# Earlier weights, a DMA transpose, one q buffer and a finer last tile in an attention and FFN kernel

## The chip, the cores and the metric

The kernel runs on one core of one Trainium2 chip. The metric is the time of one execution in device microseconds (us). "Faster" or "slower" needs 2%; everything below that is "same". TensorE (PE in the profile) does the matmuls and the PE transposes (a tile transposed by a matmul with the identity), VectorE and ScalarE the elementwise work, GpSimd (POOL in the profile) issues the loads, SyncE (SP) the stores and the DMA transposes. PSUM is the memory that TensorE writes its results to.

## The reference, cut to what matters

```python
# q, k, v: 8 batches x 8 heads x 1024 tokens x 64; E, F: 64 x 1024
k_proj = np.einsum('ks,bhsd->bhkd', E, k)            # k': 64 rows per head
v_proj = np.einsum('ks,bhsd->bhkd', F, v)
attn   = softmax(q @ k_proj.T / 8)                   # over 64 keys
x      = (attn @ v_proj)                             # to (8192 tokens, 512)
h      = x @ w_in                                    # 512 -> 2048
out    = (h * sigmoid(1.702 * h)) @ w_out            # 2048 -> 512
```

## The kernel before

The kernel works through 16 FFN blocks of 512 tokens, two for each batch. Block `j` has 16 tiles of the first matmul (`ffn1`), a Gelu on each, then 8 half steps of the second matmul (`ffn2`). Block 0 does its tiles in half width (256 tokens); the first of them compute the Gelu by way of Tanh, before ScalarE has loaded its Gelu table, and "tile 10" of the start is the eleventh of these half tiles. The attention of later blocks is cut into pieces and put between the tiles: `at(j, slot, piece)` runs a piece after a given tile of block j, and slots from `O` = 16 on lie in its second half. Loads cast from float32 to bf16 on the way and are issued by GpSimd in program order. These are the places that the change touches:

```python
def q_buf(b):                       # one buffer for batches 0 and 2, another for the rest
    t = ldpool.tile([P, J * H * D], BF16, name="q_even" if b in (0, 2) else "q_sb")
...
def load(b):                        # order in which a batch is loaded
    for what in ("kvq", "kqv", "kvq", "qkv")[min(b, 4) - 1]:
...
load_kv(q, qt, 0, "", H, 2, 2)      # q's second 256 tokens, then w_in in 8 pieces
for i in range(6):
    load_w_in(i)
...
def kv_out(b):                      # k' and v' of batch b leave PSUM
        nc.vector.tensor_copy(k_b, ps[LO])
        if b > 1:                   # k' is transposed by DMA; batch 1's on TensorE
            nc.sync.dma_start_transpose(out=kts[b % 2], in_=...)
...
at(1, 10, proj(1))                  # projection of batch 1
at(1, 11, kv_out(1))
at(1, 13, lambda: k_tr(1, kbs[1], 0))          # four PE transposes
at(1, 1, q_dma(1, 0, JB), q_dma(1, JB, JB))    # q of batch 1, transposed by DMA
at(1, O + 4, q_dma(2))
at(2, 1, proj(2), kv_out(2), sums(3), spread(3))
```

At the end, the last 128 x 512 output tile is computed and stored in two halves of 256 columns, the second copied out by VectorE.

The softmax here doesn't subtract the row's maximum and nothing guards it: scores larger than these inputs give would overflow.

Of the kernel before, what the change touches and what calls it, by code (L numbers as in the profile page):

```python
# [10 lines left out]
BF16 = mybir.dt.bfloat16  # L11
# [6 lines left out]
def kernel(ctx, tc, q, k, v, E, F,  # L18
                                                     moe_w_in, moe_w_out, out):
    nc = tc.nc  # L20
    B, H, S, D = q.shape
    KP, _ = E.shape
    DM, DFF = moe_w_in.shape
# [28 lines left out]
    def load_kv(src, dst, b, name, hs=H, js=0, jn=J):  # L52
        if b not in dst:
            dst[b] = ldpool.tile([P, H, J, D], BF16, name=name)
        sv = src[b].rearrange("h (p j) d -> p h j d", p=P)
        for h, n in [(h, hs) for h in range(0, H, hs)] if isinstance(hs, int) else hs:
            nc.gpsimd.dma_start(out=dst[b][:, h:h + n, js:js + jn], in_=sv[:, h:h + n, js:js + jn])  # L57
# [1 line left out]


    def q_buf(b):
        t = ldpool.tile([P, J * H * D], BF16, name="q_even" if b in (0, 2) else "q_sb")
        order = "h j" if b == 0 else "j h"
        return t.rearrange(f"p ({order} d) -> p {order} d", d=D, h=H)

# [4 lines left out]
            nc.gpsimd.dma_start(out=qt[b][:, j], in_=qv[:, j])  # L70

    def load(b):
        for what in ("kvq", "kqv", "kvq", "qkv")[min(b, 4) - 1]:
            if what == "q":
                load_q(b)
            elif what == "k":
                load_kv(k, kt, b, "k_sb")
            else:
                load_kv(v, vt, b, "v_sb")
# [14 lines left out]
    qt[0] = q_buf(0)  # L94
    load_kv(q, qt, 0, "", H, 0, 2)
    load_kv(v, vt, 0, "v_sb", ((0, 4), (4, 2), (6, 2)))
    load_kv(q, qt, 0, "", H, 2, 2)
    for i in range(6):
        load_w_in(i)
    load_kv(q, qt, 0, "", H, JB, JB)  # L100
    for i in range(6, 8):
# [36 lines left out]
    def f_tile(shape, dt=F32):  # L138
        return ps_f.tile(shape, dt, name="f_ps")
# [24 lines left out]
        return efts[j // (J // 2)][:, j % (J // 2), cols]  # L164


    kvps, kbs, qT, expT, xT, rbc, rdens = {}, {}, {}, {}, {}, {}, {}

    def proj(b):
        def go():  # L170
# [15 lines left out]
    def k_piece(h0, n):  # L186
        k_ps = proj0(0, h0, n)
        k_b = att.tile([KP, n, D], BF16, name=f"k0_b{h0}", bufs=1)
        nc.vector.tensor_copy(k_b, k_ps[LO])
        warm(2)  # L190
        k_tr(0, k_b, h0 // 2)

    def k_tr(b, k_b, p0):
        n = k_b.shape[1] // 2
        t_ps = f_tile([P, n, KP], BF16)
        for p in range(n):
            nc.tensor.transpose(t_ps[:, p, :], k_b[:, 2 * p:2 * p + 2, :].rearrange("k t d -> k (t d)"),
                                ident[:KP, :KP])
        nc.vector.tensor_copy(kts[b % 2][:, p0:p0 + n, :], t_ps)

    def vx_of(b, p):
        if b == 1:
# [21 lines left out]
    def kv_out(b):  # L224
        def go():
            ps = kvps.pop(b)
            k_b = att.tile([KP, H, D], BF16, name="k_b")
            nc.vector.tensor_copy(k_b, ps[LO])  # L228
            if b > 1:
                nc.sync.dma_start_transpose(out=kts[b % 2], in_=k_b.rearrange("k h d -> k (h d)"))  # L230
            v_out(b, ps)
            kbs[b] = k_b
        return go

    q0s = [[consts.tile([P, 2, 2, P], BF16, name=f"q0T{g}{u}") for u in range(2)] for g in range(2)]
# [1 line left out]
    def q_tr0(g, u, cp):  # L237
        t_ps = f_tile([P, 2, 2, P], BF16)
        for jj in range(2):
            for h in range(4):  # L240
                r = h % 2 * D
                nc.tensor.transpose(t_ps[r:r + D, jj, h // 2, :], qt[0][:, 4 * u + h, 2 * g + jj, :], ident)
        cp(q0s[g][u], t_ps)
# [33 lines left out]
    def scores(h, u, half=None, x=False):  # L277
        b, c = divmod(h, NB2)
        j0, n = (c * JB, JB) if half is None else (c * JB + half * JB // 2, JB // 2)
        ts = slice(j0 * P - c * TB, (j0 + n) * P - c * TB)  # L280

        def go():
            if h not in expT:
                expT[h] = att.tile([P, HP, TB], BF16, name="expT", bufs=3)
            s_ps = [(x_tile() if x else f_tile([P, TB]))[:, :n * P] for _ in range(2)]
            eight(s_ps, [kts[b % 2][:, 2 * u + i, :] for i in range(2)],
                 [q0s[half][u][:, :, i, :] if h == 0 else qT[b][:, j0:j0 + n, 2 * u + i, :]
                   for i in range(2)])
            for i in range(2):
                nc.scalar.activation(expT[h][:, 2 * u + i, ts], s_ps[i], AF.Exp, scale=scale)  # L290
        return go
# [59 lines left out]
    def tok(h, p, half):  # L351
        def go():
            d_ps = f_tile([P, 4, D + 1]) if (h, half) == (0, 0) and p > 1 else                 ps_x.tile([P, 4, D + 1], F32, name="x_ps")
            for i in range(2):
                t = 2 * half + i
                nc.tensor.matmul(d_ps[:, 2 * i:2 * i + 2, :].rearrange("s t d -> s (t d)"),  # L356
                                 expT[h][:, p, t * P:(t + 1) * P],
                                 vx_of(h // NB2, p).rearrange("r t d -> r (t d)"),
                                 start=True, stop=True)
            rd = work.tile([P, 4, 1], F32, name="rd")  # L360
            nc.vector.reciprocal(rd, d_ps[:, :, D:])
            xs[h, p, half] = work.tile([P, 4, D], BF16, name="x_sb", bufs=4)
            nc.vector.tensor_tensor(xs[h, p, half], d_ps[:, :, :D], rd.to_broadcast([P, 4, D]), op=ALU.mult)  # L363
        return go
# [14 lines left out]
    def ffn1(j, fc, ts=slice(0, TB)):  # L379
        if j not in gts:  # L380
            gts[j] = work.tile([P, FC, TB], BF16, name="gT")
        n = ts.stop - ts.start
        h_ps = f_tile([P, n])
        for kc in range(KC):
            nc.tensor.matmul(h_ps, w_in_sb[:, kc, fc * P:(fc + 1) * P], xT[j][:, kc, ts],  # L385
                             start=(kc == 0), stop=(kc == KC - 1))
        if j > 0 or ts.start > 0 or fc > 1:
            nc.scalar.activation(gts[j][:, fc, ts], h_ps, AF.Gelu_apprx_sigmoid)  # L388
        else:

            t_sb = work.tile([P, n], F32, name="t_sb", bufs=3)
            nc.scalar.activation(t_sb, h_ps, AF.Tanh, scale=0.851)
            g = gts[j][:, fc, ts]
            nc.vector.scalar_tensor_tensor(g, t_sb, 1.0, h_ps, op0=ALU.add, op1=ALU.mult)
            nc.vector.tensor_scalar_mul(g, g, 0.5)

    def ffn2(j, n, fcs):
        b, c = divmod(j, NB2)
        ov = out[b * S:(b + 1) * S, :].rearrange("(p j) m -> p j m", j=J)
        if j not in osb:  # L400
            osb[j] = work.tile([P, JB, DM], F32, name="o_sb")
        if j == NBLK - 1 and n == JB - 1:

            if fcs.start == 0:
                for i, cp in enumerate((nc.scalar.copy, nc.vector.tensor_copy)):
                    ms = slice(i * DM // 2, (i + 1) * DM // 2)
                    l_ps = f_tile([P, DM // 2])
                    for fc in range(FC):
                        nc.tensor.matmul(l_ps, gts[j][:, fc, n * P:(n + 1) * P], w_out_sb[:, fc, ms],  # L409
                                         start=(fc == 0), stop=(fc == FC - 1))  # L410
                    cp(osb[j][:, n, ms], l_ps)  # L411
                    nc.sync.dma_start(out=ov[:, c * JB + n, ms], in_=osb[j][:, n, ms])
            return
        if fcs.start == 0:
            o_ps[n] = f_tile([P, DM])
        for fc in fcs:
            nc.tensor.matmul(o_ps[n], gts[j][:, fc, n * P:(n + 1) * P], w_out_sb[:, fc, :],  # L417
                             start=(fc == 0), stop=(fc == FC - 1))
        if fcs.stop == FC:
            nc.scalar.copy(osb[j][:, n, :], o_ps.pop(n))  # L420
            if j == NBLK - 1:
                nc.sync.dma_start(out=ov[:, c * JB + n, :], in_=osb[j][:, n, :])
            elif n == JB - 1:
                nc.sync.dma_start(out=ov[:, c * JB:(c + 1) * JB, :], in_=osb[j])
# [3 lines left out]
    def at(j, slot, *fs):  # L428
        fill.setdefault((j, slot), []).extend(fs)
# [24 lines left out]
    x_tr(0, 2, 0)()  # L454
    tok(0, 3, 0)()
    x_tr(0, 3, 0)()
    q_tr0(1, 0, DV)
    q_tr0(1, 1, DV)

    order = [(half, fc) for fcs in (range(12), range(12, FC)) for half in range(2) for fc in fcs]  # L460
    at(0, 1, scores(0, 0, 1), scores(0, 1, 1, True), gelu_table)
    for p in range(HP):
        at(0, 2 + p, tok(0, p, 1))
        at(0, 5 + p, x_tr(0, p, 1))
    at(0, 20, q_tr(2))
    at(0, 23, q_tr(3))
    for u in range(2):
# [2 lines left out]
    for p in range(HP):  # L470
        at(0, Q + (2, 4, 6, 7)[p], tok(1, p, 0), tok(1, p, 1))
        at(0, Q + (4, 6, 7, 8)[p], x_tr(1, p, 0), x_tr(1, p, 1))
    at(1, 10, proj(1))
    at(1, 11, kv_out(1))
    at(1, 13, lambda: k_tr(1, kbs[1], 0))
    at(1, 1, q_dma(1, 0, JB), q_dma(1, JB, JB))
    for u in range(2):
        at(1, O, scores(2, u, None, u > 0))
        at(2, O, scores(4, u, None, u > 0))
# [80 lines left out]
```

## Time and profile before

| what | value | where it is read |
|---|---|---|
| time | 510.91 us, median of 3 (510.8 to 511.16) | times |
| span of the profiled run | 509.6 us | head of the page |
| TensorE busy | 503.0 us | page, part 1 |
| batch 2's v: landing, first use | 89.8 us, 90.1 us | tile view, chain |
| last matmul's start to the end | 3.8 us | timeline |

The profiled execution took 511.42 us; its span is 1.8 us shorter, since it counts from the program's first instruction to its last. The lines are shown inside the prediction. One view that it tells only in words is the table of waits of TensorE from 25 to 505 us (who waited, on whom: us in total, times, longest):

```profile
PE f_ps L385 <- ACT gT L388: 0.3, 1, 0.3
PE f_ps L385 <- DMA w_in_sb<-in_moe_w_in_dram: 0.2, 1, 0.2
```

Both waits lie before 28 us. After that TensorE waits for nothing.

### The profile page before, as it was taken

The numbers are of one execution on the slowest core, as the hardware profiler recorded it, in microseconds if no ns is written. First come the engines' busy times: TensorE is split into PE (matmuls) and PEld (weight loads), VectorE is DVE, ScalarE is ACT, GpSimd is POOL, SyncE is SP. The second block draws the span as 40 slices with busy tenths as digits, with TensorE's granted clock in tenths as the row PEclk, the third lists the DMA queues.
The fourth block names the chain that finished last, engine by engine and source line by source line (L and its number), as shares of the span: only waits on it lengthen the run. The fifth ranks groups of instructions, "written<-read, shape, count | busy, mean of one in ns | idle before, by whom it ended". The sixth has DMA issues, their size and how long they took to land.

```text
span 509.6 us, 7212 instructions
## 1 busy us (share of the span) xinstructions
PE 503.0 (99%) x3082; PEld 232.2 (46%) x3082; DVE 158.2 (31%) x219; ACT 263.8 (52%) x443; POOL 78.0 (15%) x97
## 2 busy tenths in 40 slices
PE   8899999999999999999999999999999999999997
PEld 4585445444444444444444444444444444444444
DVE  4523114607151623216161330616223161611000
ACT  1675563664637365572746537374563737253451
POOL 7442051510600510041000510000000000000000
PEclk9999999999999999999999999999999999999999
DMA  9999999999999997598938969090603205050202
GB/s 167 197 202 207 210 140 170 228 207 137 179 195 266 116 213 125 141 150 98 228 54 223 103 117 228 23 227 1 171 1 85 83 20 147 1 167 1 82 1 82
DMA packets 125305, 68.71 MB, mean 135 GB/s; under 512 B 92325, under 2 KB 116133, under 8 KB 123353
## 3 DMA queue, kind: packets, MB, share of 16 engines
q0 software_dynamic: 84400, 29.37, 51.2%
q1 hardware_dynamic: 40792, 38.62, 29.9%
q8 instruction: 24, 0.39, 0.3%
q10 hardware_dynamic: 80, 0.26, 0.2%
q14 instruction: 9, 0.07, 0.0%
HBM read 72.88 MB, written 16.99 MB: 176 GB/s over the span
## 4 chain that ended last, share of the span: by engine, by line
PE 93%; DMA 4%; POOL 1%; issue 0%; DVE 0%; ACT 0%; POOLq 0%
PE f_ps L417 43%; PE f_ps L385 43%; PE f_ps L174 3%; DMA w_in_sb<-in_moe_w_in_dram 2%; DMA v_sb<-in_v_dram 2%; PE f_ps L271 2%; PE x_ps L271 1%; PE x_ps L309 1%; POOL k_sb L57 0%; PE x_ps L356 0%; PE x_ps L371 0%; PE f_ps L409 0%; PE f_ps L253 0%; POOL q_even L57 0%; POOL v_sb L57 0%
## 5 line engine op out<-in xcount | busy, mean ns | idle before, releaser
L417 PE MATMUL f_ps<-w_out_sb,gT 128*128 128x512 bf16 x1008 | 226.7, 379 | 0.0
L385 PE MATMUL f_ps<-xT,w_in_sb 128*128 128x512 bf16 (+1 forms) x1088 | 225.9, 367 | 0.7 <-ACT gT L388 0.3
L388 ACT ACTIVATE gT<-f_ps 128x512 bf16<-128x512 f32 (+1 forms) x270 | 151.7, 574 | 59.1 <-PE f_ps L385 57.8
L385 PEld LDWEIGHTS <-w_in_sb 128*128 128x128 bf16 x1088 | 105.5, 98 | 116.1 <-DMA w_in_sb<-in_moe_w_in_dram 0.9
L417 PEld LDWEIGHTS <-gT 128*128 128x128 bf16 x1008 | 95.9, 98 | 121.6 <-issue 11.8
L420 ACT COPY o_sb<-f_ps 128x512 f32<-128x512 f32 x63 | 36.9, 586 | 130.7 <-PE f_ps L417 121.0
L344 DVE TENSOR_TENSOR xT<-x_ps,rbc 128x512 bf16<-128x512 f32 x52 | 33.3, 684 | 217.5 <-PE x_ps L271 120.4
L312 DVE RECIPROCAL rden<-x_ps 128x512 f32<-128x512 f32 x26 | 85.3, 3322 | 10.4 <-PE x_ps L309 10.3
L70 POOL DMA_DIRECT2D q_sb<-in_q_dram x48 | 42.0, 905 | 151.1 <-DMA qT<-q_sb 122.3
L290 ACT ACTIVATE expT<-f_ps 128x512 bf16<-128x512 f32 (+1 forms) x58 | 30.1, 573 | 29.9 <-PE f_ps L271 29.9
L290 ACT ACT_TABLE_LOAD x13 | 16.7, 1283 | 4.7 <-PE f_ps L271 4.5
L294 ACT ACT_TABLE_LOAD x14 | 18.0, 1283 | 0.2
L228 DVE CAST k_b<-f_ps 64x512 bf16<-64x512 f32 x7 | 4.8, 683 | 38.8 <-PE f_ps L174 38.8
L57 POOL DMA_DIRECT2D k_sb<-in_k_dram x10 | 8.5, 854 | 52.4 <-PE f_ps L174 50.8
L174 PE MATMUL f_ps<-k_sb,eft 128*64 128x512 bf16 x56 | 13.4, 382 | 0.0
L174 PE MATMUL f_ps<-v_sb,eft 128*64 128x512 bf16 x56 | 13.4, 382 | 0.0
L144 PE MATMUL x_ps<-zeros 128*128 128x512 bf16 x34 | 11.7, 469 | 1.2 <-DVE zeros L115 1.2
L411 DVE COPY o_sb<-f_ps 128x256 f32<-128x256 f32 x1 | 0.4, 424 | 38.6 <-issue 38.6
L271 PE MATMUL f_ps<-qT,kt 64*32 64x512 bf16 x208 | 10.6, 386 | 0.0
L271 PE MATMUL x_ps<-expT,vq 64*32 64x512 bf16 x208 | 10.2, 378 | 0.0
L363 DVE TENSOR_TENSOR x_sb<-x_ps,rd 128x256 bf16<-128x256 f32 x22 | 9.3, 424 | 0.8
L57 POOL DMA_DIRECT2D v_sb<-in_v_dram x10 | 8.4, 840 | 7.2 <-DMA q_sb<-in_q_dram 5.2
(71 smaller groups left out, 124.5 us busy)
## 6 DMA issues: line engine op xcount, KB each, us to landing
out_dram<-o_sb SPq DMA_DIRECT2D x15, 1024.0 KB
rbc<-rdr SPq DMA_DIRECT2D x26, 512.0 KB
k_sb<-in_k_dram POOLq DMA_DIRECT2D x7, 1024.0 KB, 13.7
v_sb<-in_v_dram POOLq DMA_DIRECT2D x7, 1024.0 KB, 18.1
q_sb<-in_q_dram POOLq DMA_DIRECT2D x48, 128.0 KB, 6.2
w_in_sb<-in_moe_w_in_dram POOLq DMA_DIRECT2D x8, 256.0 KB, 12.2
w_out_sb<-in_moe_w_out_dram POOLq DMA_DIRECT2D x4, 512.0 KB, 14.7
q_even<-in_q_dram POOLq DMA_DIRECT2D x8, 128.0 KB, 10.9
```

The lines of the kernel that those rows point to most:

```text
L57: nc.gpsimd.dma_start(out=dst[b][:, h:h + n, js:js + jn], in_=sv[:, h:h + n, js:js + jn])
L70: nc.gpsimd.dma_start(out=qt[b][:, j], in_=qv[:, j])
L174: nc.tensor.matmul(kvps[b][r], eft(j, slice(e * KP, (e + 1) * KP)), (kt, vt)[e][b][:, :, j, :], start=(j == 0), stop=(j == J - 1))
L271: nc.tensor.matmul(outs[i][r.start + c:r.start + c + 32], lhsTs[i][ri, c:c + 32], rhss[i][ri], start=True, stop=True)
L290: nc.scalar.activation(expT[h][:, 2 * u + i, ts], s_ps[i], AF.Exp, scale=scale)
L294: nc.scalar.preload_act_table(AF.Gelu_apprx_sigmoid)
L312: nc.vector.reciprocal(rden[:, e, :], d_ps[e])
L344: nc.vector.tensor_tensor(x_of(h)[:, 2 * u + i, :], n_ps[i], rbc[h][:, 2 * u + i, :], op=ALU.mult)
L385: nc.tensor.matmul(h_ps, w_in_sb[:, kc, fc * P:(fc + 1) * P], xT[j][:, kc, ts], start=(kc == 0), stop=(kc == KC - 1))
L388: nc.scalar.activation(gts[j][:, fc, ts], h_ps, AF.Gelu_apprx_sigmoid)
L417: nc.tensor.matmul(o_ps[n], gts[j][:, fc, n * P:(n + 1) * P], w_out_sb[:, fc, :], start=(fc == 0), stop=(fc == FC - 1))
L420: nc.scalar.copy(osb[j][:, n, :], o_ps.pop(n))
```

## The change

Four parts. **Start**: w_in's first piece is loaded ahead of q's second piece so that the FFN can begin earlier; q's transposes, the Gelu table and the token steps move behind it. **k'**: batch 1's k' is transposed by DMA, which saves four PE transposes, and its projection moves from tile 10 to tile 1. **q buffer**: from batch 1 on there is one q buffer, and batch 2 is loaded q, k, v instead of k, q, v. **Tail**: the last tile comes in parts of 256, 128 and 128 columns.

```diff
-        t = ldpool.tile([P, J * H * D], BF16, name="q_even" if b in (0, 2) else "q_sb")
+        t = ldpool.tile([P, J * H * D], BF16, name="q0_sb" if b == 0 else "q_sb")
-        for what in ("kvq", "kqv", "kvq", "qkv")[min(b, 4) - 1]:
+        for what in ("kvq", "qkv", "kvq", "qkv")[min(b, 4) - 1]:
+    load_w_in(0)
     load_kv(q, qt, 0, "", H, 2, 2)
-    for i in range(6):
+    for i in range(1, 6):
...
-            if b > 1:
-                nc.sync.dma_start_transpose(out=kts[b % 2], in_=...)
+            nc.sync.dma_start_transpose(out=kts[b % 2], in_=...)
...
-        if j > 0 or ts.start > 0 or fc > 1:      # Gelu; the tiles before it use Tanh
+        if j > 0 or ts.start > 0 or fc > 3:
...
-                for i, cp in enumerate((nc.scalar.copy, nc.vector.tensor_copy)):
+                for m0, m, cp in ((0, 2, nc.vector.tensor_copy), (2, 1, nc.vector.tensor_copy), (3, 1, nc.scalar.copy)):
...
-    q_tr0(1, 0, DV)
-    q_tr0(1, 1, DV)
-    at(0, 1, scores(0, 0, 1), scores(0, 1, 1, True), gelu_table)
+    at(0, 1, lambda: q_tr0(1, 0, DV), lambda: q_tr0(1, 1, AC))
+    at(0, 2, scores(0, 0, 1), scores(0, 1, 1, True))
+    at(0, 3, gelu_table)
...                                              # tok and x_tr: two slots later
-    at(1, 10, proj(1))
-    at(1, 11, kv_out(1))
-    at(1, 13, lambda: k_tr(1, kbs[1], 0))
-    at(1, 1, q_dma(1, 0, JB), q_dma(1, JB, JB))
+    at(1, 1, proj(1), kv_out(1))
+    at(1, 2, q_dma(1, 0, JB), q_dma(1, JB, JB))
```

More of the change, by code (lines that the diff above doesn't have):

```diff
@@ L164, in eft @@
         return efts[j // (J // 2)][:, j % (J // 2), cols]
-    kvps, kbs, qT, expT, xT, rbc, rdens = {}, {}, {}, {}, {}, {}, {}
+    kvps, qT, expT, xT, rbc, rdens = {}, {}, {}, {}, {}, {}
     def proj(b):
@@ L190, in k_piece, with k_tr @@
         warm(2)
-        k_tr(0, k_b, h0 // 2)
-    def k_tr(b, k_b, p0):
+        k_tr(k_b, h0 // 2)
+    def k_tr(k_b, p0):
         n = k_b.shape[1] // 2
@@ L198, in k_tr @@
                                 ident[:KP, :KP])
-        nc.vector.tensor_copy(kts[b % 2][:, p0:p0 + n, :], t_ps)
+        nc.vector.tensor_copy(kts[0][:, p0:p0 + n, :], t_ps)
     def vx_of(b, p):
@@ L228, in go @@
             nc.vector.tensor_copy(k_b, ps[LO])
-            if b > 1:
-                nc.sync.dma_start_transpose(out=kts[b % 2], in_=k_b.rearrange("k h d -> k (h d)"))
+            nc.sync.dma_start_transpose(out=kts[b % 2], in_=k_b.rearrange("k h d -> k (h d)"))
             v_out(b, ps)
-            kbs[b] = k_b
         return go
@@ L404, in ffn2 @@
             if fcs.start == 0:
-                for i, cp in enumerate((nc.scalar.copy, nc.vector.tensor_copy)):
-                    ms = slice(i * DM // 2, (i + 1) * DM // 2)
-                    l_ps = f_tile([P, DM // 2])
+                for m0, m, cp in ((0, 2, nc.vector.tensor_copy), (2, 1, nc.vector.tensor_copy), (3, 1, nc.scalar.copy)):
+                    ms = slice(m0 * DM // 4, (m0 + m) * DM // 4)
+                    l_ps = f_tile([P, m * DM // 4])
                     for fc in range(FC):
@@ L456 @@
     x_tr(0, 3, 0)()
-    q_tr0(1, 0, DV)
-    q_tr0(1, 1, DV)
     order = [(half, fc) for fcs in (range(12), range(12, FC)) for half in range(2) for fc in fcs]
-    at(0, 1, scores(0, 0, 1), scores(0, 1, 1, True), gelu_table)
+    at(0, 1, lambda: q_tr0(1, 0, DV), lambda: q_tr0(1, 1, AC))
+    at(0, 2, scores(0, 0, 1), scores(0, 1, 1, True))
+    at(0, 3, gelu_table)
     for p in range(HP):
-        at(0, 2 + p, tok(0, p, 1))
-        at(0, 5 + p, x_tr(0, p, 1))
+        at(0, 4 + p, tok(0, p, 1))
+        at(0, 7 + p, x_tr(0, p, 1))
     at(0, 20, q_tr(2))
```

## The prediction

> **What bounds the kernel now.** I read the page first. Its first part says that TensorE is busy for 503.0 of 509.6 us, and the chain that ended last is almost all TensorE:
>
> ```profile
> PE 503.0 (99%) x3082; PEld 232.2 (46%) x3082; DVE 158.2 (31%) x219; ACT 263.8 (52%) x443; POOL 78.0 (15%) x97
> ...
> PE 93%; DMA 4%; POOL 1%; issue 0%; DVE 0%; ACT 0%; POOLq 0%
> ```
>
> So a part of the change can only pay by removing TensorE instructions, or one of the 6.6 us (509.6 - 503.0) in which TensorE is idle. The table of waits says where those are: nothing at all between 60 and 505 us, 1.2 us before the first matmul, 3.5 us after the last one, and under 2 us of small gaps before 28 us. Some 500 us in the middle have no slack; equally, any new wait there is added to the end in full. I then read the chain in order of time, at the three places that the change touches (start us, length us, what):
>
> ```profile
> 16.40 11.50 DMA w_in_sb<-in_moe_w_in_dram
> 27.90 0.05 issue
> 27.95 4.98 PE f_ps L385 x44
> ...
> 69.39 0.22 PE f_ps L197 x4
> ...
> 90.11 1.85 PE f_ps L174 x16
> ...
> 506.18 0.42 DVE o_sb L411
> ```
>
> The reader should see four things. The front of the kernel is tied to the sixth piece of w_in, which lands at 27.90. The four PE transposes of batch 1's k' cost 0.22 us on the chain. Batch 2's projection starts at 90.11. And the end hangs on one 0.42 us VectorE copy and the store after it.
>
> Next I read the GpSimd and SyncE timelines between 55 and 95 us, because the change moves loads there:
>
> ```profile
> 57.47 7.03 SPq L261 DMA_TRANSPOSE qT<-q_sb  x2
> 84.59 6.84 SPq L261 DMA_TRANSPOSE qT<-q_even  x1
> ...
> 66.99 0.87 POOL L57 DMA_DIRECT2D k_sb<-in_k_dram  x1 [12.31 <-PE f_ps L174]
> 67.86 6.13 POOL L70 DMA_DIRECT2D q_even<-in_q_dram  x7
> 77.99 0.88 POOL L70 DMA_DIRECT2D q_even<-in_q_dram  x1 [4.00 <-DMA k_sb<-in_k_dram]
> 79.18 0.87 POOL L57 DMA_DIRECT2D v_sb<-in_v_dram  x1 [0.32 <-issue]
> ```
>
> The tile view of v_sb, confined to that last issue, gives its time to landing:
>
> ```profile
> DMA to landing us min/median/max: 10.6/10.6/10.6
> ```
>
> So batch 2's v lands at 79.18 + 10.6 = 89.8, and the projection that reads it starts at 90.11. **The old kernel has only 0.3 us to spare there.** That is the most important number for this change.
>
> **What the Trainium skill says.** (1) "TensorE: Matmul & The Clock Gate", section "Back-to-back issue gap": about N/2.4 + 2.5 ns from one matmul to the next, so 56 ns for 128 columns and 109 ns for 256. The trace agrees: 8 matmuls of 128 columns start 56 ns apart at 18.1 us, and those of 256 columns 109 ns apart. (2) "ScalarE: Activation LUTs", "What ACT_TABLE_LOAD costs": 1283 ns, and a drain of about 1380 ns. The trace has the 1.28 us (23.82 to 25.11), but the next ACTIVATE starts within 0.02 us, so I count no drain. (3) "DMA: Bandwidth & Descriptors", "Queues, rings and completion order": each DMA engine takes turns between the queues that have work for it, packet by packet. The trace fits: see rival B. (4) the first page again, "What's actually happening": an idle window of about 3.4 us halves the clock. No wait before is that long, so this trace does not show it.
>
> **Part 1, the start.** All loads before 60 us come one after another at the queue's pace: the w_in pieces land 1.34 us apart. q's second piece lands at 19.85 and w_in's first at 21.19. Swapped, w_in's first lands near 18.7 and q's second near 21.2. Everything after keeps its place, so w_in's sixth piece still lands at 27.9. The first FFN block may start at 20.4 rather than 21.23, but the 16 transposes of q and their copies (0.72 us) only move behind it, and tiles 10 and 11 still wait until 27.9. So nothing is gained at the start. Something may be lost, and I worked it out engine by engine from the durations of before. The Gelu table now comes after four Tanh tiles, one 0.58 us copy and four Exp (1.05 us): ScalarE loads it near 25.2 instead of 23.82, so the first Gelu starts near 26.5 instead of 25.12. VectorE has two more Tanh tiles of about 0.65 us, ahead of the first token normalisation, which slips from 23.5 to about 25.9. TensorE then waits for x_sb and for a free PSUM buffer, and reaches tile 10 near 28.0; before, it was ready at 27.63 and waited 0.32 for the load. Also, the last transpose of x (0.11 us) now stands behind tile 10. Sum: **+0.2 us** (0.1 to 0.5).
>
> **Part 2, k' of batch 1 by DMA.** Four PE transposes go: **-0.22 us**. The projection moves from tile 10 to tile 1 of its block, to about 57.1. Its k lands at 48.5 (28.44 + 20.1) and its v at 53.5 in the tile views, so it need not wait. VectorE finishes k' near 59.8; the DMA transposes follow, k' 1.2 us of issue and q 5 to 7. Both are needed only by the scores at 73.1, so they are in time.
>
> **Part 3, one q buffer.** Batch 2's q may now be loaded only when batch 1's q transposes are done. The order q, k, v puts k and v behind that wait. Step by step: q's transposes are issued from about 61.0. The undisturbed one at 121.5 moved its data at 217 KB/us, so 1 MB takes 4.8 us, from about 62.2 to 67.0. GpSimd was then released 1.2 to 1.4 us after the last data in three later batches, so at **68.4** (66.99 before). Eight q issues of 0.87 take 7.0; the last q piece lands 10.6 after the start (as it did twice later, 168 and 223 us), at 79.0. k and v then need 5.1 us each (the pace of batch 1's), undisturbed: k at 84.1, **v at 89.2 at best**. TensorE asks for it at 90.11 + 0.2 - 0.22 = 90.1. So without a collision there is no wait.
>
> **Part 4, the tail.** TensorE's time hardly changes: 16 x 109 + 32 x 56 = 3.54 us against 32 x 109 = 3.49. The copy after the last matmul becomes a 128-column ScalarE copy. ScalarE copies 512 columns in 0.58 and 256 in 0.37, so 128 take about 0.27, against 0.42: -0.15. The last store has half the bytes; the old one's packets ran over 0.52 us, so perhaps -0.2. Sum: **-0.3 us**.
>
> Without new waits: +0.2 - 0.22 - 0.3 = -0.3, so 510.6.
>
> **Rival A: everything is hidden and the time is 510.3 to 510.9.** For it: the best-case v landing, 89.2, is ahead of 90.1, and the parts that remove work are certain. Against it: the margin is 0.9 us after a chain of six estimates.
>
> **Rival B: batch 2's k and v collide with batch 2's q transposes.** Before, the transposes at 84.59 met only the end of v. Now they are issued when q has landed, near 79.0, just as k begins, and their data come 1.2 to 2.7 us later, over most of the load of k and v. How the two share is seen at 245 to 247 us, where batch 6's k load meets a k' transpose, against 85 to 87 where a load is alone (queue, packets, MB, share):
>
> ```profile
> q0 software_dynamic: 401, 0.41, 124.0%
> ...
> q0 software_dynamic: 214, 0.22, 93.9%
> q1 hardware_dynamic: 193, 0.05, 44.0%
> ```
>
> The first line is the load alone, 0.205 MB per us; the other two are the mixture, where it gets about half. At 80.2 to 81.7 some 1.4 to 1.7 MB of the 2 MB of k and v (as written) remain. At 125 to 150 KB/us they take 9 to 13 us: v lands at 90 to 95, and TensorE waits **0 to 5 us, most likely about 2**. If the wait passed 3 us the clock might drop too, for a further 1 to 2 us. For it: the measured mixture. Against it: that sample has other small traffic in it and only 64 KB of transposes.
>
> **Rival C: ScalarE becomes the bound of the start.** If Tanh, Exp and table load take longer than I counted, tile 10 starts near 28.7: +0.8 in place of +0.2. It cannot grow further, for a half-width Gelu takes 0.27 to 0.33 us against 0.44 of matmuls, so ScalarE catches up.
>
> **Range and chances.** A has about 40%, B in some strength 60%. Their mixture has its middle near 1 us over the old time: 510.91 - 0.3 + 1.3 = **511.9 us**. The low end, 510.1, is A with a better tail and start; the high end, 515.8, is B with a wait of 5 us. Two per cent is 10.2 us: a gain of that size has nowhere to come from, and a loss needs a wait three times the size that I expect. Chances: faster 0.01, same 0.96, slower 0.03.
>
> **What would show it right or wrong.** Start: the eleventh FFN tile starts at 27.9 to 28.3, with the sixth piece of w_in at 27.9 still. Middle: GpSimd's first batch 2 q issue at about 68.4, and the table of waits has a new row between 60 and 505 us, the projection (or its weight load) waiting for v_sb; its length separates A from B. Tail: about 3.2 us from the last matmul to the end instead of 3.5. I am wrong if batch 2's v lands before 90 with the transposes running, if the first 28 us shrink by more than 0.3 us, or if a wait appears at the scores of batch 1 or 2.

## The result and the profile after

The changed kernel takes **515.15 us** (median of 6, 513.94 to 516.63), the kernel before in the same rounds 510.86 (510.71 to 511.37). The ratio is 1.0084, 95% interval 1.0063 to 1.0106: "same" by the 2% rule, and clearly not faster. A ratio here is the mean time of one kernel's fast runs over that of the other's of the same rounds, so it is not quite the ratio of the medians.

The profiled execution (513.94 us, the fastest of the six, span 512.2) shows where it went. First the page, parts 1 and 4:

```profile
PE 497.8 (97%) x3043; PEld 232.1 (45%) x3094; DVE 159.0 (31%) x222; ACT 264.3 (52%) x444; POOL 78.0 (15%) x97
...
PE 87%; DMA 8%; POOL 2%; issue 1%; SPq 1%; DVE 0%; ACT 0%; POOLq 0%
```

TensorE's share of the chain fell and DMA's doubled. (Line numbers shift by one between the kernels: the projection is L174 before and L175 here. The busy sum can't be compared to 503.0: this trace lacks 51 of 3094 matmul records, weight loads against matmuls, and the table of waits shows such holes as "issue".) The table of waits of TensorE from 25 to 505 us:

```profile
PE f_ps L416 <- issue: 3.6, 23, 0.2
PE f_ps L175 <- DMA v_sb<-in_v_dram: 2.8, 1, 2.8
PE x_ps L370 <- DVE x_sb L362: 0.3, 1, 0.3
```

The second row is new: the projection (L175) waits 2.8 us for v. The SyncE and GpSimd timelines from 56 to 110 us, and below them the landing of that v load from its tile view:

```profile
59.91 1.26 SPq L230 DMA_TRANSPOSE kt<-k_b  x1
61.36 32.27 SPq L260 DMA_TRANSPOSE qT<-q_sb  x3
...
68.67 7.00 POOL L70 DMA_DIRECT2D q_sb<-in_q_dram  x8 [14.06 <-DMA qT<-q_sb]
75.59 0.94 POOL L57 DMA_DIRECT2D k_sb<-in_k_dram  x1
76.45 0.95 POOL L57 DMA_DIRECT2D v_sb<-in_v_dram  x1
...
DMA to landing us min/median/max: 16.6/16.6/16.6
```

Loading starts at 68.67, once batch 1's q transposes are done; v is issued 2.7 us earlier than before (76.45, not 79.18), yet lands 3.3 us later: 76.45 + 16.6 = 93.1, against 89.8. The last of the three qT transposes in the second line, batch 2's, is issued at 79.37 and runs beside k and v. The DMA view from 85 to 90 us (queue, packets, MB, share of time) says how the two shared the engines; q0 is the loads, q1 the transposes:

```profile
DMA packets 1536, 0.98 MB, mean 196 GB/s; under 512 B 772, under 2 KB 1536, under 8 KB 1536
q0 software_dynamic: 770, 0.78, 91.7%
q1 hardware_dynamic: 766, 0.20, 29.6%
```

In 5 us there are 770 packets of one and 766 of the other: they go turn by turn. But a load's packet has 1 KB and a transpose's 256 B, so the loads fall to 0.78 / 5 = 0.156 MB per us (0.205 alone, in the prediction's lines) and the transposes to 0.04 (alone, in the kernel before, 0.217 at 123 to 127 us and 0.29 at 90 to 92).

The balance of this execution, from the start of the same weight loads in both traces (the columns give the time, in us, at which each stretch ends):

| stretch | before | after | adds |
|---|---|---|---|
| start, to the first tile of block 1 | 54.98 | 55.18 | +0.20 |
| to the second half of block 1 | 71.07 | 70.95 | -0.32 |
| to tile 2 of block 2 (behind the projection) | 92.23 | 95.29 | +3.18 |
| to block 15 | 478.05 | 481.11 | 0.00 |
| from there to the end | 509.65 | 512.17 | -0.54 |
| sum | | | +2.52 |

The wait costs 3.18 us and is listed as 2.8, because the list counts from the modelled end of k's first matmul, which starts at 89.92 and is 0.40 us long; v's first, which before started together with it, starts at 93.14, 3.2 us later. The other five executions took up to 2.7 us more than this one; the run that repeats the changed kernel shows why.

### The profile page after: what moved, and what is told of

Same layout as the page of the kernel before. It is cut to its first block, busy times and chain, and to the rows that moved or that the text cites. A ratio compares the mean times of both kernels' runs of the same rounds, so it can differ in the third digit from the quotient of the medians.

```text
span 512.2 us, 7200 instructions
## 1 busy us (share of the span) xinstructions
PE 497.8 (97%) x3043; PEld 232.1 (45%) x3094; DVE 159.0 (31%) x222; ACT 264.3 (52%) x444; POOL 78.0 (15%) x97
## 4 chain that ended last, share of the span: by engine, by line
PE 87%; DMA 8%; POOL 2%; issue 1%; SPq 1%; DVE 0%; ACT 0%; POOLq 0%
PE f_ps L384 40%; PE f_ps L416 40%; DMA v_sb<-in_v_dram 3%; PE f_ps L175 3%; DMA w_in_sb<-in_moe_w_in_dram 2%; PE f_ps L270 2%; DMA k_sb<-in_k_dram 1%; POOL q_sb L70 1%; PE x_ps L270 1%; DMA qT<-q_sb 1%; PE f_ps L408 1%; PE x_ps L308 1%; SPq L260 0%; POOL k_sb L57 0%; PE x_ps L370 0%
## 5 line engine op out<-in xcount | busy, mean ns | idle before, releaser
L416 PE MATMUL f_ps<-w_out_sb,gT 128*128 128x512 bf16 x975 | 220.6, 379 | 4.2 <-issue 3.6
L70 POOL DMA_DIRECT2D q_sb<-in_q_dram x56 | 49.0, 904 | 162.8 <-DMA qT<-q_sb 137.2
L289 ACT ACT_TABLE_LOAD x13 | 16.7, 1283 | 4.7 <-PE f_ps L270 4.5
L293 ACT ACT_TABLE_LOAD x14 | 18.0, 1283 | 0.3
L175 PE MATMUL f_ps<-v_sb,eft 128*64 128x512 bf16 x56 | 13.4, 381 | 2.8 <-DMA v_sb<-in_v_dram 2.8
L175 PE MATMUL f_ps<-k_sb,eft 128*64 128x512 bf16 x56 | 13.6, 382 | 0.0
L360 DVE RECIPROCAL rd<-x_ps 128x4 f32<-128x4 f32 x22 | 4.0, 180 | 24.2 <-PE x_ps L355 24.2
L175 PEld LDWEIGHTS <-eft 128*64 128x64 bf16 x112 | 6.0, 109 | 10.2 <-issue 6.1
L270 PE MATMUL x_ps<-expT,vq 64*32 64x512 bf16 x208 | 10.2, 378 | 0.0
```

The lines of the kernel that those rows point to most:

```text
L70: nc.gpsimd.dma_start(out=qt[b][:, j], in_=qv[:, j])
L175: nc.tensor.matmul(kvps[b][r], eft(j, slice(e * KP, (e + 1) * KP)), (kt, vt)[e][b][:, :, j, :], start=(j == 0), stop=(j == J - 1))
L270: nc.tensor.matmul(outs[i][r.start + c:r.start + c + 32], lhsTs[i][ri, c:c + 32], rhss[i][ri], start=True, stop=True)
L289: nc.scalar.activation(expT[h][:, 2 * u + i, ts], s_ps[i], AF.Exp, scale=scale)
L293: nc.scalar.preload_act_table(AF.Gelu_apprx_sigmoid)
L416: nc.tensor.matmul(o_ps[n], gts[j][:, fc, n * P:(n + 1) * P], w_out_sb[:, fc, :], start=(fc == 0), stop=(fc == FC - 1))
```

## The experiments

Twelve runs, the last but one of them the changed kernel again, were made in four groups; each group had its own runs of before on its chip. All gave correct results. By the 2% rule late_q is "unclear" (its interval spans 1.02) and all the others are "same"; where the text below calls one slower, its interval lies above 1.

| run | median us | before us | ratio (95%) |
|---|---|---|---|
| late_q | 520.38 | 511.03 | 1.0189 (1.0175 to 1.0203) |
| two_q | 512.33 | 511.03 | 1.0024 (1.0011 to 1.0036) |
| start_only | 512.31 | 511.03 | 1.0018 (1.0006 to 1.0031) |
| tail_only | 510.90 | 511.03 | 0.9997 (0.9985 to 1.0010) |
| kvq_order | 518.14 | 511.57 | 1.0120 (1.0106 to 1.0135) |
| new_lateproj | 512.66 | 511.57 | 1.0022 (1.0010 to 1.0034) |
| old_kvq_tail | 512.89 | 511.57 | 1.0027 (1.0011 to 1.0044) |
| old_kvq_tail_kdma | 511.73 | 511.57 | 1.0000 (0.9988 to 1.0012) |
| old_early_kdma_tail | 511.36 | 511.45 | 0.9998 (0.9985 to 1.0010) |
| kdma_only | 512.51 | 511.45 | 1.0019 (1.0005 to 1.0032) |
| after_again | 516.64 | 511.45 | 1.0098 (1.0076 to 1.0119) |
| old_early_tail | 510.77 | 511.28 | 0.9988 (0.9974 to 1.0001) |

### Is it the collision or the late start of the loads? (late_q)

```diff
-    at(1, O + 4, q_dma(2))
-    at(2, 1, proj(2), kv_out(2), sums(3), spread(3))
+    at(2, 1, proj(2), kv_out(2), q_dma(2), sums(3), spread(3))
```

> The changed kernel, with one thing moved: batch 2's q transposes are issued after batch 2's projection (tile 1 of the block at 90 us) and no longer as soon as q has landed at 79 us. One q buffer and the order q, k, v stay. Collision theory (my rival B): k and v now load alone at about 205 KB/us instead of 155, v lands near 89, the 2.8 us wait of the projection for v_sb falls to under 0.5 us, and the time is 510.4 to 511.0 us, with little scatter. Rival theory (v is late only because the one q buffer delays the start of the loads to 68.7 us): v still lands after 91.5, a wait of over 1.5 us stays, and the time is above 512.5 us.

The waits of TensorE and the landing of v (tile view):

```profile
PE f_ps L270 <- DMA qT<-q_sb: 6.1, 1, 6.1
PE f_ps L416 <- issue: 3.8, 23, 0.3
PE f_ps L175 <- DMA v_sb<-in_v_dram: 1.0, 1, 1.0
...
DMA to landing us min/median/max: 14.9/14.9/14.9
```

The wait for v fell from 2.8 to 1.0 us, and v landed at 91.4 instead of 93.1 (one profiled execution of each). So 1.8 us of the wait are the collision, and 1.0 us remains without it: both theories hold a part, mine the larger. k landed at 86.3 in both, 2 us later than I had worked out, in late_q with no transpose in flight at all. The DMA view of late_q, from the landing of q's last piece to that of k (79.4 to 86.4 us) and from there to that of v (to 91.4), tells part of the reason:

```profile
q0 software_dynamic: 1285, 1.30, 118.4%
q0 software_dynamic: 698, 0.70, 84.0%
```

A load of 1 MB is 1024 packets of 1 KB, so a third of v's had moved when k landed: the two loads overlap. What was slow is the pair, 12.0 us where I had counted 10.2, at 0.186 and then 0.14 MB per us and not 0.205. Why, I did not settle.

I had not asked what the moved transposes would meet. They met the next batch's k and v: SyncE needed 15.96 us to issue them (6.84 in the kernel before), and the scores that read them waited 6.1 us. The time that I expected for this run, about 510.7, is therefore far off, and its cause is the same collision at another place. A second loss follows. The windows view around that wait (stretch, its length, PE busy, ..., granted clock of TensorE with 1.00 for full speed, DMA share, GB/s):

```profile
110.00:113.00 3.00, 0.00 (x0) 0.00 (x0) 0.00 (x0) 0.00 (x0) 0.00 (x0) 0.58 1.26 253
113.00:116.00 3.00, 1.93 (x26) 0.67 (x28) 0.00 (x0) 1.54 (x2) 1.55 (x2) 0.50 0.25 82
116.00:120.00 4.00, 4.00 (x17) 1.73 (x16) 0.00 (x0) 2.39 (x5) 4.00 (x6) 0.84 1.12 209
```

During the wait the clock falls to half, and it stays there for a while after work has begun again.

### Two q buffers again (two_q), and k and v ahead of q (kvq_order)

```diff
 # two_q
-        ... name="q0_sb" if b == 0 else "q_sb")        ("kvq", "qkv", "kvq", "qkv")
+        ... name="q_even" if b in (0, 2) else "q_sb")  ("kvq", "kqv", "kvq", "qkv")
 # kvq_order (one buffer)
-        for what in ("kvq", "qkv", "kvq", "qkv")[min(b, 4) - 1]:
+        for what in ("kvq", "kvq", "kvq", "qkv")[min(b, 4) - 1]:
```

> The changed kernel with part 3 undone: batches 0 and 2 share a q buffer of their own again, and batch 2 loads in the order k, q, v. If the one q buffer is all that was wrong, time 510.4 to 511.0. My theory says that the collision only moves: the projection of batch 1 is now at 57 us, so batch 2's loads start near 60 us and meet batch 1's q transposes, which then get some 40 KB/us instead of 217 while the loads last; the scores of batch 1 at about 73 us need the first half of them (0.5 MB after 64 KB of k'), so I expect a wait of 1 to 6 us there and 511.5 to 517 us.

> The changed kernel with batch 2 loaded in the order k, v, q; everything else stays (one q buffer, projection of batch 1 at tile 1). k and v no longer stand behind the wait for the q buffer, so they load from about 59 us and the wait of batch 2's projection for v_sb (2.8 us) should go to 0. Theory of the collision: they now meet batch 1's q transposes (61 to 68 us in the changed kernel), which lose their speed until the loads end near 72 us, so a wait of 1 to 4 us for qT appears at the scores of batch 1 (about 73 us), as it did with two q buffers (1.6 us); 511.5 to 514.5 us. Theory that only the q buffer's wait in front of k and v costs time: no wait after 30 us and 510.4 to 511.2.

In both the wait for v is gone, and the wait of batch 1's scores for their transposed q is there in its place; 1.6 us with two buffers:

```profile
PE f_ps L270 <- DMA qT<-q_sb: 1.6, 1, 1.6
```

two_q also shows what is shared. From 71 to 73 us these transposes run beside q's pieces, which come in packets of 128 bytes (DMA view: queue, packets, MB, share):

```profile
q1 hardware_dynamic: 828, 0.21, 82.2%
q0 software_dynamic: 827, 0.10, 79.2%
```

The packets are again equal in number, but here the transposes get 0.105 MB per us, more than twice what they got beside packets of 1 KB. The turns are by packet, so the larger packet takes the larger share.

With k and v first (kvq_order) the wait for qT is 6.1 us, and the chain shows what it was (start us, length us, what):

```profile
62.10 17.71 DMA qT<-q_sb
79.81 0.14 issue
79.94 0.63 PE f_ps L270 x8
```

In the changed kernel, where nothing loads beside them, both halves of these transposes are through 6.8 us after the first issue (61.36 to 68.1); here, beside k and v, the first half alone takes 17.7. two_q fell within its range, kvq_order is 3.6 us above the top of its: I had sized the wait at 1 to 4 us, and had not counted that the clock falls to 0.50 during it (windows view) and returns only near 83 us, 3 us after work has begun again, which costs some 1.5 us more. The theory that only the q buffer costs time would have put both near 511.

### The start alone (start_only), the tail alone (tail_only)

Both are the kernel before with that part of the change's diff alone.

> The kernel before with part 1 alone: w_in's first piece earlier, q transposes behind two FFN tiles, four Tanh tiles, the Gelu table and the token steps two tiles later. My prediction: +0.2 us (0.1 to 0.5), so 511.0 to 511.4 beside a before of 510.9; TensorE leaves the first twelve half tiles about 0.2 us later. Rival (the part helps, as it was meant to): 0.3 us or more below before.

> The kernel before with part 4 alone: the last output tile in parts of 256, 128 and 128 columns. My prediction: -0.3 us (0.15 from the copy, up to 0.2 from the store), 510.5 to 510.7 beside 510.9; 3.2 us from the last matmul to the end. Rival (a third store in the queue, or the end set by a fixed landing time): no change, or +0.1.

**start_only** is slower by 0.18% (0.06 to 0.31), more than I expected. In its profile the first tile of block 1 begins at 55.28 (54.98 before): +0.3. On top, its projection of batch 2 waits 0.5 us for v. v's load was issued 0.4 us later (79.59, not 79.18) and landed at 91.2, 1.4 us later, for the last q pieces ahead of it were slow in this execution. That is the 0.3 us of slack of the kernel before being used up: any lateness ahead of this point can appear as a wait for v.

**tail_only**: the last matmul starts at 505.89 and the program ends at 509.13, so 3.24 us, against 3.83 before. (The 3.2 of my prediction counted from that matmul's end, as its 3.5 for the kernel before did; counted so, the changed kernel has 3.0.) The copies, from the timelines of before and then of tail_only:

```profile
504.38 0.37 ACT L411 COPY o_sb<-f_ps 128x256 f32<-128x256 f32 x1 [1.16 <-PE f_ps L409]
506.18 0.42 DVE L411 COPY o_sb<-f_ps 128x256 f32<-128x256 f32 x1 [38.63 <-issue]
```

```profile
504.42 0.42 DVE L411 COPY o_sb<-f_ps 128x256 f32<-128x256 f32 x1 [36.88 <-issue]
505.25 0.29 DVE L411 COPY o_sb<-f_ps 128x128 f32<-128x128 f32 x1 [0.41 <-PE f_ps L409]
506.15 0.27 ACT L411 COPY o_sb<-f_ps 128x128 f32<-128x128 f32 x1 [2.95 <-PE f_ps L409]
```

The last copy takes 0.27 and no longer 0.42. The tail's stretch is 0.59 us shorter in the profile, but the ratio, 0.9997, cannot tell 0.6 us (0.12%) from nothing: its interval is 0.25% wide. A reason for such scatter is visible in most of these traces: the first matmuls on k wait for its load, and this wait is 0.2 us in one execution and 1.9 in another.

### A placement without collisions? (new_lateproj, old_kvq_tail, old_kvq_tail_kdma)

```diff
 # new_lateproj: the changed kernel with
-    at(1, 1, proj(1), kv_out(1))
-    at(1, 2, q_dma(1, 0, JB), q_dma(1, JB, JB))
+    at(1, 10, proj(1))
+    at(1, 11, kv_out(1))
+    at(1, 1, q_dma(1, 0, JB), q_dma(1, JB, JB))      # and batch 2 loaded k, v, q
 # old_kvq_tail: the kernel before, batch 2 loaded k, v, q, and the new tail
 # old_kvq_tail_kdma: the same, and k' of batch 1 by DMA instead of k_tr
```

> The changed kernel with batch 1's projection back at tiles 10 and 11, its q transposes ahead of it at tile 1, and batch 2 loaded k, v, q. One q buffer stays. Now no load meets a large transpose: q transposes of batch 1 from 57 to 65 us, k and v of batch 2 from 67 to 79, q after them, its transposes near 87, needed at 104. Theory of the collision: no wait for v_sb or qT between 30 and 505 us, and 510.5 to 511.0 us: the start's +0.3 against the tail and the four PE transposes. A risk: k' of batch 1 is now transposed near 68 us while k of batch 2 begins to load, and is needed at 73. If the single q buffer is bad in itself, a wait of over 1 us for q or qT stays.

> The kernel before with two things: batch 2 loaded in the order k, v, q (v then lands near 79 us, 11 us before it is read, not 0.3), and the tail in three parts. Expected 510.4 to 510.7, and less scatter than before (whose slower runs I suspect of a short wait for v); the tail's -0.2 to -0.4 is most of it.

> The same, and batch 1's k' transposed by DMA with its projection still at tiles 10 and 11: the four PE transposes (0.22 us) go, so 510.2 to 510.5, if k' (64 KB, issued near 67.5 us) lands before the scores at 73 us although k of batch 2 loads at the same time. If the collision slows even 64 KB, a wait of up to 2 us for kt appears there and it is slower than the one without.

No large wait is left in any, which fits the theory: with q's transposes clear of the loads, the waits for v and qT are gone with one q buffer as with two. But each has a wait for kt, the small transpose of k' (64 KB): 1.2 us at batch 1's scores in new_lateproj and in old_kvq_tail_kdma, and in old_kvq_tail, where batch 1's k' is on TensorE, at batch 2's scores near 108 us:

```profile
PE f_ps L271 <- DMA kt<-k_b: 1.9, 1, 1.9
```

There SyncE, which works in order, had q's transposes of batch 2 and a store ahead of k' (issued at 95.89, in the kernel before at 92.74), so that k' met the load of batch 3's k. In this trace the store's own 1 MB also moves on the transposes' queue from 100 to 105 us, ahead of k' (105 to 108); how much of the 1.9 us is the store and how much the load was not separated. All three missed what I expected for the whole by 1.2 to 2.2 us; 0.7 of that is this chip's (before took 511.57 there, 510.86 in the first rounds). The rest is of the order of these waits for kt: a small transpose, which I had taken to be harmless.

### k' by DMA alone (kdma_only), earlier (old_early_kdma_tail), and the repetition (after_again)

```diff
 # kdma_only: the kernel before with
-            if b > 1:
-                nc.sync.dma_start_transpose(out=kts[b % 2], in_=...)
+            nc.sync.dma_start_transpose(out=kts[b % 2], in_=...)
-    at(1, 13, lambda: k_tr(1, kbs[1], 0))
 # old_early_kdma_tail: the same with the new tail, and
-    at(1, 10, proj(1))
-    at(1, 11, kv_out(1))
+    at(1, 8, proj(1))
+    at(1, 9, kv_out(1))
```

> The kernel before with batch 1's k' by DMA and nothing else (projection at tiles 10 and 11 as before). My prediction counted -0.22 us for the four PE transposes and no wait. After the last runs I expect instead a wait of about 1.2 us for kt at the scores near 73 us, since k' is issued at 67.5 us and meets batch 2's k load: +0.5 to +1.3 us net.

> The kernel before (its start, two q buffers, order k, q, v) with the tail in three parts, batch 1's k' by DMA, and batch 1's projection two tiles earlier, at 8 and 9. By the collision theory this is the place where a DMA transpose of k' fits: it is issued near 66 us, behind q's transposes (data until 66.6 us) and ahead of the first data of batch 2's k (two tiles earlier than before, near 67.3). Then kt lands before 70 and no wait for it appears at 73 us, where the version with the projection at tile 10 waited 1.2 us; v of batch 2 also lands 1 us earlier. Expected 0.4 to 0.9 us below before of the same chip. If 64 KB still collide, a wait of 0.5 us or more for kt and no gain.

> The changed kernel unaltered, on the same chip as the other two. Its runs so far lie at 513.9 to 516.6 and those above 515 have a granted clock of 0.996 to 0.997, not 0.999. I expect the same split: a wait for v_sb of 2.5 to 4 us, and a lower mean clock exactly in the runs that are over 4 us slower than before[...] (the 6.1 us wait of the late-q run was followed by a granted clock of 0.58 and 0.50). If the profile shows the wait elsewhere, my account of the slower runs is wrong.

The chain of **kdma_only** shows the small transpose:

```profile
66.97 6.80 DMA kt<-k_b
73.77 0.04 issue
73.81 0.41 PE f_ps L270 x8
```

It takes 6.8 us and costs a wait of 1.5 us; the four PE transposes that it replaces cost 0.22. In **old_early_kdma_tail** k' is issued 1.4 us earlier and lands at the same 73.77, after 8.23 us. Its first packets do not move until batch 2's k has begun to load, 3.5 us after the issue. The q transposes ahead of it end at 66.5 us, and from there to 69 us the engines move only 29 to 82 GB/s. My expectation that it would slip in ahead of the load was wrong, and I can't say what holds it back. In the changed kernel k' is issued at 59.91, away from loads, and no wait for kt appears. So what makes k' by DMA pay there is the early projection, and the early projection is what brings the transposes and loads of batch 2 into each other's way.

**after_again** explains the scatter. Its profiled execution (517.09 us, span 515.3) waits 3.1 us for v, and then:

```profile
94.00:96.00 2.00, 1.29 (x12) 0.83 (x13) 0.00 (x0) 0.00 (x0) 0.00 (x0) 1.00 1.27 230
96.00:98.00 2.00, 2.00 (x15) 0.47 (x12) 0.88 (x2) 0.00 (x0) 1.02 (x2) 0.50 1.12 398
98.00:100.00 2.00, 2.00 (x8) 0.77 (x7) 1.96 (x3) 0.54 (x1) 1.99 (x3) 0.65 0.87 222
```

The clock is at 0.50 and 0.65 for 4 us, a loss of 2 x 0.50 + 2 x 0.35 = 1.7 us. In the earlier profile, with a wait listed as 2.8 us, it stays at 1.00. The weight loads behind the wait, in the earlier profile and then in this one, show in brackets how long no weights were loaded:

```profile
93.14 1.40 PEld L175 LDWEIGHTS <-eft 128*64 128x64 bf16 x14 [3.11 <-issue]
94.71 1.45 PEld L175 LDWEIGHTS <-eft 128*64 128x64 bf16 x14 [3.35 <-issue]
```

Both gaps are a little below the 3.4 us that the prediction cites from the skill. The two executions show that the longer gap cost clock and the shorter did not; where a limit lies they do not show. The span is 3.1 us longer than in that profile: 1.3 from a later start (the first tile of block 1 at 56.51, not 55.18; the first k load was waited for 1.9 us, not 0.4), 0.3 from the wait and 1.7 from the clock make 3.3. Of the six runs here, the one with a mean clock of 1.000 took 514.6, and the five with 0.993 to 0.997 took 516.1 to 517.9, as expected.

### The parts that stand (old_early_tail)

```diff
 # the kernel before with the new tail, and
-    at(1, 10, proj(1))
-    at(1, 11, kv_out(1))
-    at(1, 13, lambda: k_tr(1, kbs[1], 0))
+    at(1, 8, proj(1))
+    at(1, 9, kv_out(1))
+    at(1, 11, lambda: k_tr(1, kbs[1], 0))
```

> The kernel before with the two parts that the runs so far leave standing: the tail in three parts, and batch 1's projection two tiles earlier (8 and 9, the four PE transposes of k' at 11) so that batch 2's v lands near 88 us and not 89.8. k' stays on TensorE. Expected: no wait for kt, qT or v_sb between 30 and 505 us, 3.2 us from the last matmul to the end instead of 3.8, and 0.3 to 0.7 us below before of the same chip. If the tail's gain does not reach the whole, as in the tail run alone (ratio 0.9997), it is the same as before.

As in the kernel before, nothing waits after 28 us (a first row of "issue" is again holes of the trace), and the median is 510.77 against 511.28 for before (ratio 0.9988, 0.9974 to 1.0001), well below the changed kernel. It has the lowest ratio of all that I ran, and is still "same": the interval just includes 1.

## Why the prediction was right, point by point

The measured 515.15 lies within the range of 510.1 to 515.8, near its upper end, and "same" was the likely one. The cause, the collision of rival B, was named; that the number fell inside the range is partly luck, for two errors of opposite sign met in it (part 3 and rival B below). By the prediction's own steps:

- **Part 1, +0.2 us: right.** The trace shows +0.20. The Gelu table is loaded at 25.18 (25.2 predicted) and the first Gelu starts at 26.47 (26.5); the sixth piece of w_in still lands at 27.8, and tile 10 starts at 28.0. Starting the FFN 0.9 us earlier gained nothing because a later piece sets the pace. Alone, in another execution, it cost 0.3 us, and 0.5 us more by way of v.
- **Part 2, -0.22 us: right in sign and near in size here, for a reason that I had not seen.** The stretch is 0.32 us shorter, 0.10 more than the four transposes, which I did not explain. But kdma_only is slower than before. The DMA transpose is free only because the projection moved away from the loads as well.
- **Part 3, start of the loads at 68.4: right** (68.67), and q's last piece at 79.0 (79.22). **"v at 89.2 at best": off by 2.2 us.** Without a collision v landed at 91.4 (late_q). The mis-sized term is the load of k and v behind q: 10.2 us predicted for the two (5.1 each), 12.0 measured in late_q; k landed 6.9 to 7.1 us after q, with a part of v moved among it. So rival A's world did not exist: even undisturbed, TensorE would have waited 1.0 us.
- **Rival B, a wait of about 2 us: it is what happened**, 2.8 to 3.1 us. The mixture gave the loads 156 KB/us where I said 125 to 150. (My sample of 2 us took in stretches in which little moved at all; its first half microsecond alone has 73 packets, 0.15 MB per us.) The transposes' data began at 83, not at 80.2 to 81.7. Both made the collision milder than I feared, and the slow loads of part 3 made up for it. late_q, two_q and kvq_order move the collision and show the wait following it.
- **"If the wait passed 3 us the clock might drop too": it did** in after_again (3.1 listed, 0.50 granted). It is the smaller part of why the median is above my 511.9: the fastest execution, with a mean clock of 0.999, is already 2.0 us above, and the median lies 1.2 above that one. The larger part is that the middle of my mixture gave 40% to no wait at all, and 2 us to it otherwise; the wait was in both of the profiles of this kernel, and cost 3.2 us in the first.
- **"A loss needs a wait three times the size that I expect": a wrong sum.** 10.2 us of loss would need a wait of 10.5, five times the 2 us. Nothing hung on it.
- **Part 4, -0.3 us: right in sign, too small.** It is -0.54 in the changed kernel's balance and 0.59 in the tail alone, 0.15 of it the copy. From the last copy's end to the end of the program it is 3.05 us in the kernel before and 2.71 in tail_only (lines above), so the smaller last store and what follows it are most of the rest.
- **Rival C: fell.** Tile 10 starts at 28.0, not 28.7.

## What to carry to other kernels

Before moving a DMA transpose or a load, draw what the other queue does in the same microseconds: beside loads of 1 KB packets, the transposes here ran at a fifth of their speed or less, and the loads at three quarters of theirs; beside packets of 128 bytes the transposes ran at half. When an engine is busy for 99% of the span, look for the smallest margin between a landing and its use (0.3 us here) and ask which part of a change spends it. And a wait that moves is not a wait removed: four variants of the changed kernel (late_q, two_q, kvq_order, new_lateproj) only handed it to another reader.

## What the Trainium skill lacked or had wrong

- "DMA: Bandwidth & Descriptors", section "Rules for kernel authors": "A transpose next to ordinary DMAs needs nothing". The results were correct, so it holds for that. The page gives no rates for the mixture: 156 KB/us for the loads (205 alone) and 40 for the transposes (217 to 290 alone), and 6.8 us for 64 KB. The turn-taking of the section "Queues, rings and completion order" fits the counts, 770 packets against 766 and, in two_q, 828 against 827; here a turn is one packet of the trace, of 1 KB, 256 B or 128 B.
- "ScalarE: Activation LUTs", section "What ACT_TABLE_LOAD costs": the 1283 ns agree, the drain of about 1380 ns does not show; in the changed kernel the first Gelu starts 0.01 us after the load (25.18 + 1.28, then 26.47).
- No page tells why two loads of 1 MB behind 128-byte packets took 12.0 us together and not 10.2, nor what holds a small transpose back for 3.5 us when a load is about to begin.
